# A spectral layer and two expert layers on one core: x in runs of 2 KB, eleven chunks and thirteen decode steps ahead of the second stage

## The chip, the cores and the metric

The kernel runs on one core of a Trainium2 chip. The core has TensorE (PE, the matrix engine), VectorE (DVE), ScalarE (ACT), GpSimd (POOL) and SyncE (SP), which here only issues DMAs, and 16 DMA engines. TensorE writes to PSUM (8 banks of 128 partitions), the other engines compute from PSUM and SBUF. The metric is the device time of one execution in microseconds. The kernel before took 1226.06 us, the median of three runs (1225.86 to 1226.39).

## The reference

x has 2 batches of 3008 positions and 256 features. Each batch goes through a Fourier transform over the positions, a complex linear layer with bias, a soft shrink, and the transform back; then two expert layers follow on all 6016 rows.

```python
X = np.fft.rfft(x, axis=1)
Yr = Xr @ w_r - Xi @ w_i + b_r            # Xr, Xi: real and imaginary part, float32
Yi = Xr @ w_i + Xi @ w_r + b_i
Yr = np.sign(Yr) * np.maximum(np.abs(Yr) - 0.01, 0.0)      # Yi likewise
y = np.fft.irfft(Yr + 1j * Yi, n=3008, axis=1).reshape(6016, 256)
h = y @ moe_w_in;   y = (h - np.tanh(h)) @ moe_w_out        # w_in 256 x 2048, w_out 2048 x 256, float64
h = y @ moe2_w_in;  out = (h * np.clip(h + 3, 0, 6) / 6) @ moe2_w_out
```

## The kernel before

The transform is split as 3008 = 47 x 64 into small matrix products. **First stage (dft_a, L262).** x of a batch lies as 94 rows of 32 positions (a row is 32 KB). A chunk is 4 positions of every row; there are 8 chunks per batch, numbered 0 to 15 over both. dft_a multiplies a chunk from the left with a 96 x 96 matrix (`amt`): four float32 matmuls of 256 columns, two to a PSUM bank; ScalarE copies the two banks back over the chunk (L279) and stores the chunk to `s1` in DRAM from its own queue (L280). The chunks of batch 0 have eight tiles (`xa`), those of batch 1 a ring of three (`xb`).

**Second stage (L674 on, steps t = 0 to 23).** It works on pairs of frequency rows. dft_b (L292) reads a group of `s1` (load_bi, L284, a group serves two steps) and multiplies with `bmt`; ScalarE and VectorE split the result into a high and a low part (`fh`, `fl`); linear (L322) multiplies with the high and low parts of w_r and w_i in three passes, 24 matmuls; the shrink (L337) is three operations of VectorE with ScalarE's copy `sh` (L350) and VectorE's rest `sl` (L354) behind; dft_c (L356) is the third transform, two steps behind linear, and goes to `s2` in DRAM. A step t holds linear(t), dft_c(t-2), dft_b(t+2) and, as long as there are chunks left, the dft_a of one chunk of batch 1: in the kernel before chunks 0 to 7 are done ahead of the stage and chunk 8 + t in steps 0 to 7. Steps 17 to 20 also hold the first dft_d (L394), the fourth transform, for the first tile of the expert layers, and steps 19 to 23 its splits and subtractions (`cmL`, `b22l`, L407, L423).

**The decode (w_steps, L163).** The expert weights come as float64. A generator turns one 256 x 256 block after the other into a high and a low float32 part: raw words in (`raw`, a ring of three), ScalarE's two copies (L172, L173) to `ws`, VectorE's mask (L175), shift (L185), rounding (L197) and, for w_in, four sums (L201 to L205), then ScalarE's high part (L182) and VectorE's low part (L190). Every `next` does one of some six small pieces; each block's third piece issues the load of a later block. In the second stage four calls are made in every step from step 2 on, until 13 blocks are done. The remaining blocks are decoded during the first expert tile.

**Expert layers.** 16 tiles of 376 rows, eight for each layer, each in eight groups of products in three passes; this is most of the time, from some 250 us to the end.

**What sets the order.** The schedule is manual: each engine runs its instructions in the order in which the program writes them. An instruction waits in its queue for what it needs, and everything behind it on its engine waits as well. SyncE issues most DMAs, ScalarE the stores of s1, GpSimd the loads of `cm`, each after a one-element copy to `gate` (L617) that waits for a given tile. Eight semaphores serve the DMAs of SyncE and ScalarE in turn, so an issue can also wait for an earlier transfer on its semaphore.

Of the kernel before, what the change touches and what calls it, by code (L numbers as in the profile page):

```python
# [10 lines left out]
F32 = mybir.dt.float32  # L11
# [3 lines left out]
ACTF = mybir.ActivationFunctionType  # L15
# [72 lines left out]
def spectral_moe_kernel(ctx: ExitStack, tc: tile.TileContext, x, w_r, w_i, b_r, b_i,  # L88
# [14 lines left out]
    y1d = dr.tile([8, 128, 4, 376], F32, name="y1d")  # L103
    s1 = [s1[b].rearrange("k r n d -> k (r n) d") for b in range(2)]
    s2 = [s2[b].rearrange("k r n d -> k (r n) d") for b in range(2)]
    s1w = [s.rearrange("k (q j) d -> (k q) j d", j=32) for s in s1]
    s2w = [s.rearrange("k (q j) d -> (k q) j d", j=32) for s in s2]

    def bank(tag):
# [21 lines left out]
    def alloc_w(nm, c):  # L131
# [3 lines left out]
        W[nm, c] = pl.tile([128, 2, n], F32R, tag=f"w{kind}{c}", name=f"w{kind}{c}")  # L135
        return W[nm, c]

    NDEC, NST = 13, 2
    w_src = {"1i": w1i, "1o": w1o, "2i": w2i, "2o": w2o}
    w_order = [(nm, c) for c in range(8) for nm in ("1i", "1o")]  # L140
    w_order += [(nm, c) for nm in ("2i", "2o") for c in range(8)]
    w_raw = {}
    ptr = {"load": 0, "dec": 0}
# [68 lines left out]
    def w_step():  # L212
        next(w_gen, None)
# [25 lines left out]
    wa_cm = tc.tile_pool(name="wa", bufs=1, side="right")  # L239
    wa = wa_cm.__enter__()  # L240
    x0 = [wa.tile([128, 4, D], F32, name=f"xa{r}") for r in range(8)]
    stores = []

    def load_x(i):
        if i >= 16:
            return
        b, c = divmod(i, 8)
        if b == 0:
            v = x.rearrange("b s d -> (b s) d")[0:96 * 32].rearrange("(r j) d -> r j d", j=32)
            sp.dma_start(out=x0[c][0:96], in_=v[:, 4 * c:4 * c + 4, :])  # L250
        else:
            v = x[b].rearrange("(r j) d -> r j d", j=32)[:, 4 * c:4 * c + 4, :]
            for r0, r1 in ((0, 80), (80, 94)):
                sp.dma_start(out=x1[c % 3][r0:r1], in_=v[r0:r1])

# [5 lines left out]
    def dft_a(i, finish=True):  # L261
        b, c = divmod(i, 8)  # L262
        xt = (x1[c % 3] if b else x0[c])[0:96]
        banks_ = []
        for g in range(2):
            p = bank("acc" if i < 8 and i % 2 else "h")
            pv = p[0:96].rearrange("p (u d) -> p u d", d=D)
            for u in range(2):
                pe.matmul(out=pv[:, u, :], lhsT=amt, rhs=xt[:, 2 * g + u, :], start=True, stop=True)
            banks_.append(pv)  # L270
        if finish:
            dft_a_out(i, banks_)
        return banks_

    def dft_a_out(i, banks_):
        b, c = divmod(i, 8)
        xt = (x1[c % 3] if b else x0[c])[0:96]
        for g in range(2):
            act.activation(out=xt[:, 2 * g:2 * g + 2, :], in_=banks_[g], func=ACTF.Copy)  # L279
        act.dma_start(out=s1w[b][:, 4 * c:4 * c + 4, :], in_=xt)  # L280

    bi_t, xf_t, s_t = {}, {}, {}
    GB = 4
# [1 line left out]
    def load_bi(i):  # L285
        if i >= 2 * K1 // GB:
            return
        b, g = divmod(i, K1 // GB)
        t = bi_ring[i % 3]
        sp.dma_start(out=t, in_=s1[b][g * GB:(g + 1) * GB].rearrange("k p d -> p k d"))  # L290
        bi_t[i] = t
# [316 lines left out]
    with tc.manual_schedule():  # L608
        bv = bm.rearrange("p (k f) -> p k f", k=K1)

        def load_bm(g):
            if g < 6:
                sp.dma_start(out=bmt[:, 4 * g:4 * g + 4, :], in_=bv[:, 4 * g:4 * g + 4, :])

        def load_cm(g, after):
            if g < 6:
                pool.tensor_copy(out=gate[0:1, 0:1], in_=after)  # L617
                for h, t in enumerate((cmH, cmL)):
                    pool.dma_start(out=t[:, 512 * g:512 * g + 512], in_=cm[:, h, 512 * g:512 * g + 512])

        sp.dma_start(out=amt, in_=am)
        for i in range(8):
            load_x(i)
        for r in range(3):
            pool.memset(x1[r][64:96], 0.0)
        dve.memset(three, 3.0)
        lws = []
        for w in (w_r, w_i):
            t = wl.tile([128, 2, D], F32, tag="ly", name="lwf")
            sp.dma_start(out=t, in_=w.rearrange("(h p) d -> p h d", p=128))  # L630
            lws.append(t)
        load_bm(0)
        sp.dma_start(out=dmt, in_=dm)
        for k, w in enumerate((b_r, b_i)):
            sp.dma_start(out=bias[64 * k:64 * k + 64, 0, :],
                         in_=w.rearrange("(o d) -> o d", o=1).broadcast_to([64, D]))
        for i in range(8):
            dft_a(i)
        load_x(8)
        load_bi(0)  # L640
        load_x(9)
        load_bi(1)
        load_bm(1)
        load_cm(0, x0[7][0:1, 3, 0:1])
        load_x(10)
        w_load()
        wa_cm.__exit__(None, None, None)
        wpool["r"] = ctx.enter_context(tc.tile_pool(name="wr", bufs=1, side="right", reuse_waits="tile"))
        for k in range(2):
            split(lwH[:, k], lwL[:, k], lws[k])  # L650
        for j in range(2):
            dft_b(j)
            evict_b_hi(j)
            evict_b_lo(j)
            evict_b_neg(j)
        load_bi(2)
        NP = K1
        a_next = 8
        for t in range(NP):
            linear(t)  # L660
            if t > 1:
                dft_c(t - 2)
            if t + 2 < NP:
                dft_b(t + 2)
            ab = dft_a(a_next, False) if a_next < 16 else None
            if t > 1:
                evict_c(t - 2)
            if t + 2 < NP:
                evict_b_hi(t + 2)
            shrink(t)  # L670
            shrink_hi(t)
            if t + 2 < NP:
                evict_b_lo(t + 2)
            if t == NP - 1:  # L674
                first = first_group()
                next(first)
            if t + 2 < NP:
                evict_b_neg(t + 2)
            for _ in range(2):
                if t > 1 and ptr["dec"] < NDEC:  # L680
                    w_step()
            shrink_lo(t)
            for nm in {20: ("b11", "b21"), 21: ("t1",), 22: ("t2", "b22")}.get(t, ()):
                op_lo(0, nm)
            if t == 20:
                op_sub(T1, B12, B11, dve)
            if t == 21:
                op_sub(T2, B22, T1, dve)
            if ab:
                dft_a_out(a_next, ab)  # L690
                a_next += 1
            flush_stores()
            if t % 2 == 0:
                load_bm(t // 2 + 2)
                load_cm(t // 2 + 1, s_t[t][0].bitcast(F32)[0:1, 0, 0:1])
            if t > 0:
                load_x(10 + t)
            if t in (0, 1):
                w_load()
            if t % 2 == 1:  # L700
                load_bi((t + 1) // 2 + 2)
            for _ in range(NST):
                if t > 1 and ptr["dec"] < NDEC:
                    w_step()
            if t == 14:
                load_din(0, din0)
            if t == 15:
                load_din(1, x1[2])
            if t in (17, 18):
                dft_d(0, t - 17, "h")  # L710
            if t in (19, 20):
                dft_d(1, t - 19, "h")
            for nm in {19: ("b11", "b21"), 20: ("t1",), 21: ("t2", "b22")}.get(t, ()):
                op_hi(0, nm)
            if t == 22:
                op_sub(T3, B22, B12)
                op_sub(T4, B21, T2)
# [110 lines left out]
```

## Time and profile before

| | |
|---|---|
| profiled execution, own time | 1225.78 us |
| its span, first to last instruction | 1224.0 us |
| TensorE busy | 1183.5 us (97%) |
| VectorE busy | 962.5 us (79%) |
| ScalarE busy | 880.8 us (72%) |
| GpSimd busy | 158.7 us (13%) |
| DMA traffic | 96.51 MB, mean 79 GB/s |

The profile is one execution of the program. Busy shares are means over stages that are limited by different things, so the table says little by itself; the rows further down take the stages apart. A row of the timeline gives start and duration of instructions, and in brackets how long the engine had been idle and what ended that. A row of the table of windows gives, for a stretch of time, what each engine was busy with in it, TensorE's granted clock as a share of full speed, the DMA engines' busy share and the rate.

### The profile page before, as it was taken

How to read it: one execution, taken by the hardware profiler on the slowest of the kernel's cores; microseconds unless marked ns; L12 is line 12 of the kernel's file. 1: busy time of each engine (PE TensorE's matmuls, PEld its weight loads, DVE VectorE, ACT ScalarE, POOL GpSimd, SP SyncE). 2: the span in 40 equal slices, each digit the busy share in tenths (PEclk: the TensorE clock that was granted, in tenths of full speed). 3: DMA queues.
4: the chain of work that ended last, by engine and by line, in shares of the span. 5: the costliest groups of instructions: out<-in, count | busy, mean ns of one | idle time of the engine just before them, and what ended most of it. 6: DMA issues, size and time to landing. Idle time of an engine off the chain costs nothing.

```text
span 1224.0 us, 20880 instructions
## 1 busy us (share of the span) xinstructions
PE 1183.5 (97%) x7824; PEld 1163.0 (95%) x7824; DVE 962.5 (79%) x1808; ACT 880.8 (72%) x1836; POOL 158.7 (13%) x164
## 2 busy tenths in 40 slices
PE   5899979899999999999999999999999999999998
PEld 3799969899999999999999999999999999999998
DVE  0479988888888888888778787878787878787875
ACT  3477767777787777777777777777777777777775
POOL 1000010201102020202021320202020202020200
PEclk9899989999999999999999999999999999999999
DMA  9896522232212122211104530101010101001000
GB/s 269 239 334 209 185 86 67 99 106 74 74 49 98 66 69 69 61 60 44 43 1 166 185 130 1 51 1 52 1 52 1 52 1 35 18 22 31 10 18 26
DMA packets 47797, 96.51 MB, mean 79 GB/s; under 512 B 4448, under 2 KB 27488, under 8 KB 47696
## 3 DMA queue, kind: packets, MB, share of 16 engines
q1 hardware_dynamic: 41728, 74.08, 18.8%
q0 software_dynamic: 4032, 14.68, 3.9%
q10 hardware_dynamic: 1936, 6.42, 1.4%
q8 instruction: 61, 1.00, 0.3%
q14 instruction: 40, 0.33, 0.1%
HBM read 58.73 MB, written 36.44 MB: 78 GB/s over the span
## 4 chain that ended last, share of the span: by engine, by line
PE 76%; DVE 10%; ACT 10%; issue 3%; DMA 2%; SPq 0%; ACTq 0%; DVEq 0%
PE acc L119 13%; PE acc L121 13%; PE acc L120 13%; PE al L119 7%; PE al L120 6%; PE al L121 6%; PE be L121 3%; PE be L120 3%; PE be L119 3%; ACT gh L115 2%; DVE g L440 2%; PE ga L398 2%; PE ga L120 2%; PE ga L121 2%; PE ga L119 1%
## 5 line engine op out<-in xcount | busy, mean ns | idle before, releaser
L116 DVE TENSOR_TENSOR gl<-g,gh 128x376 fp32r<-128x376 f32 x509 | 290.4, 571 | 149.7 <-ACT gh L115 122.1
L115 ACT ACTIVATE gh<-g 128x376 fp32r<-128x376 f32 x509 | 263.5, 518 | 185.5 <-DVE g L443 91.8
L121 PE MATMUL acc<-wo,gl 128*128 128x256 f32 (+1 forms) x768 | 215.9, 281 | 0.0
L120 PE MATMUL acc<-wo,gh 128*128 128x256 f32 (+1 forms) x768 | 215.8, 281 | 0.0
L119 PE MATMUL acc<-wo,gh 128*128 128x256 f32 (+1 forms) x768 | 215.7, 281 | 0.0
L119 PE MATMUL acc<-gh,wo 128*128 128x376 f32 x512 | 173.2, 338 | 0.0
L121 PE MATMUL acc<-gh,wo 128*128 128x376 f32 x512 | 171.0, 334 | 0.0
L120 PE MATMUL acc<-gl,wo 128*128 128x376 f32 x512 | 170.7, 333 | 0.0
L120 PEld LDWEIGHTS acc<-wo,gh 128*128 128x128 f32 (+1 forms) x768 | 143.0, 186 | 0.0
L121 PEld LDWEIGHTS acc<-wo,gl 128*128 128x128 f32 (+1 forms) x768 | 143.0, 186 | 0.0
L119 PEld LDWEIGHTS acc<-wo,gh 128*128 128x128 f32 (+1 forms) x768 | 142.8, 186 | 0.0
L407 POOL TENSOR_TENSOR bmt<-bmt 128x376 f32<-128x376 f32 x62 | 73.9, 1192 | 521.5 <-ACT bmt L400 396.8
L443 DVE SCALAR_TENSOR_TENSOR g<-e,c 128x376 f32<-128x376 f32 x192 | 119.3, 621 | 12.5 <-ACT e L442 7.9
L442 ACT ACTIVATE e<-c,three 128x376 f32<-128x376 f32 x192 | 116.7, 608 | 8.0 <-DVE c L589 7.2
L440 DVE TENSOR_TENSOR g<-c,e 128x376 f32<-128x376 f32 x189 | 113.9, 603 | 8.2 <-ACT e L439 6.0
L423 POOL TENSOR_TENSOR cmL<-bmt,cmH 128x376 fp32r<-128x376 f32 x60 | 66.1, 1102 | 325.8 <-ACT cmH L418 322.5
L439 ACT ACTIVATE e<-c 128x376 f32<-128x376 f32 x189 | 97.5, 516 | 7.9 <-DVE c L589 7.7
L119 PEld LDWEIGHTS acc<-gh,wo 128*128 128x128 f32 x512 | 96.4, 188 | 0.0
L120 PEld LDWEIGHTS acc<-gl,wo 128*128 128x128 f32 x512 | 96.3, 188 | 0.0
L121 PEld LDWEIGHTS acc<-gh,wo 128*128 128x128 f32 x512 | 96.1, 188 | 0.0
L119 PE MATMUL al<-cmH,wi 128*128 128x376 f32 x256 | 87.8, 343 | 6.3 <-ACT bi_all L538 2.9
L579 ACT ACTIVATE s<-be 128x376 f32<-128x376 f32 x127 | 61.9, 487 | 39.8 <-PE be L121 39.4
(164 smaller groups left out, 2830.8 us busy)
## 6 DMA issues: line engine op xcount, KB each, us to landing
raw<-in_moe_w_in_dram SPq DMA_DIRECT2D x16, 512.0 KB, 5.0
raw<-in_moe_w_out_dram SPq DMA_DIRECT2D x16, 512.0 KB, 4.4
w2id<-wout SPq DMA_DIRECT2D x8, 896.0 KB, 4.3
wi<-w2id POOLq DMA_DIRECT2D x8, 896.0 KB, 4.9
bi_all<-s SPq DMA_DIRECT2D x12, 512.0 KB, 6.5
y1d<-y SPq DMA_DIRECT2D x32, 188.0 KB, 2.0
bmt<-y1d SPq DMA_DIRECT2D x8, 752.0 KB, 4.9
s<-co SPq DMA_DIRECT2D x23, 256.0 KB, 5.5
```

The source lines that it names most:

```text
L115: act.activation(out=hi, in_=src, func=ACTF.Copy)
L116: (lo_eng or dve).tensor_tensor(out=lo, in0=src, in1=hi.bitcast(F32), op=ALU.subtract)
L119: pe.matmul(out=out_ap, lhsT=lh, rhs=rh, start=start, stop=False, **kw)
L120: pe.matmul(out=out_ap, lhsT=lh, rhs=rl, start=False, stop=False, **kw)
L121: pe.matmul(out=out_ap, lhsT=ll, rhs=rh, start=False, stop=stop, **kw)
L407: eng.tensor_tensor(out=out, in0=a, in1=b, op=ALU.subtract)
L423: (eng or dve).tensor_tensor(out=l, in0=OPS[nm][0], in1=h.bitcast(F32), op=ALU.subtract)
L439: act.activation(out=e, in_=src, func=ACTF.Tanh)
L440: dve.tensor_tensor(out=g, in0=src, in1=e, op=ALU.subtract)
L442: act.activation(out=e, in_=src, func=ACTF.Relu, bias=three)
L443: dve.scalar_tensor_tensor(out=g, in0=e, scalar=6.0, in1=src, op0=ALU.min, op1=ALU.mult)
L579: act.activation(out=s5, in_=be, func=ACTF.Copy)
```

## The change

- **Runs of 2 KB.** A chunk is now 2 + 2 positions of every row, 16 positions apart, instead of 4 neighbouring ones. Loads of x and stores to s1 move two runs of 2 KB, 16 KB apart, where they moved one of 4 KB.
- **Evictions.** For chunks 0 to 10 ScalarE copies one bank and VectorE the other.
- **Warm-up.** Four matmuls on a zeroed tile stand ahead of the first dft_a.
- **Eleven chunks ahead.** Chunks 8, 9 and 10 are done ahead of the second stage (A0 = 11), chunks 11 to 15 in steps 0 to 4.
- **Thirteen decode steps ahead.** Nine calls stand around chunks 8 to 10, four behind the first two dft_b. So that only tiles are used that exist by then, the order of blocks is now 1i0, 1i1, 1o0, 1o1.
- **Loads.** The first raw load and chunks 8 and 9 are issued ahead of the first stage's wait, behind w_r and w_i; chunk 10, the second raw and group 2 of s1 close behind the first group; `dm` later. The gate of the first cm load names chunk 8's tile.
- The split of w_r and w_i stands behind chunk 4.

```diff
-    s1w = [s.rearrange("k (q j) d -> (k q) j d", j=32) for s in s1]
+    s1w = [s.rearrange("k (q h j) d -> (k q) h j d", h=2, j=16) for s in s1]
...
+    A0 = 11
-    w_order = [(nm, c) for c in range(8) for nm in ("1i", "1o")]
+    w_order = [("1i", 0), ("1i", 1), ("1o", 0), ("1o", 1)]
+    w_order += [(nm, c) for c in range(2, 8) for nm in ("1i", "1o")]
...
-            sp.dma_start(out=x0[c][0:96], in_=v[:, 4 * c:4 * c + 4, :])
+            sp.dma_start(out=x0[c][0:96], in_=v[:, :, 2 * c:2 * c + 2, :])
...
-            act.activation(out=xt[:, 2 * g:2 * g + 2, :], in_=banks_[g], func=ACTF.Copy)
-        act.dma_start(out=s1w[b][:, 4 * c:4 * c + 4, :], in_=xt)
+            if g and i < A0:
+                dve.tensor_copy(out=xt[:, g], in_=banks_[g])
+            else:
+                act.activation(out=xt[:, g], in_=banks_[g], func=ACTF.Copy)
+        act.dma_start(out=s1w[b][:, :, 2 * c:2 * c + 2, :], in_=xt)
...
+        warm = ca.tile([128, 256], F32, name="warm")
+        dve.memset(warm, 0.0)
+        for _ in range(4):
+            p = bank("h")
+            pe.matmul(out=p[:, 0:256], lhsT=warm[:, 0:128], rhs=warm, start=True, stop=True)
...
+        w_load()
+        load_x(8)
         load_bm(0)
-        sp.dma_start(out=dmt, in_=dm)
+        load_x(9)
...
         for i in range(8):
             dft_a(i)
-        load_x(8)
+            if i == 4:
+                for k in range(2):
+                    split(lwH[:, k], lwL[:, k], lws[k])
         load_bi(0)
-        load_x(9)
+        load_x(10)
         load_bi(1)
+        w_load()
         load_bm(1)
-        load_cm(0, x0[7][0:1, 3, 0:1])
-        load_x(10)
+        load_cm(0, x1[0][0:1, 1, 1, 0:1])
+        load_bi(2)
         w_load()
+        sp.dma_start(out=dmt, in_=dm)
+        for i in range(8, A0):
+            w_step()
+            dft_a(i)
+            w_step()
+            w_step()
...
-        for k in range(2):
-            split(lwH[:, k], lwL[:, k], lws[k])
+        load_x(11)
         for j in range(2):
             dft_b(j)
             evict_b_hi(j)
             evict_b_lo(j)
             evict_b_neg(j)
-        load_bi(2)
+            w_step()
+            w_step()
...
-        a_next = 8
+        a_next = A0
...
-            if t > 0:
-                load_x(10 + t)
-            if t in (0, 1):
-                w_load()
+            load_x(12 + t)
```

Three places in the engines' orders. SyncE's queue at the start of the second stage, before (bi_all is a group of s1, xb a chunk of batch 1 in two parts, bmt and bias are constants, raw a block of expert weights):

```order
L635 DMA bias<-in_b_i_dram 64x256
L254 DMA xb_98<-in_x_dram 80x1024
L254 DMA xb_98<-in_x_dram 14x1024
L290 DMA bi_all<-s_0_60 128x4x256
L254 DMA xb_99<-in_x_dram 80x1024
L254 DMA xb_99<-in_x_dram 14x1024
L290 DMA bi_all<-s_0_60 128x4x256
L613 DMA bmt<-in_bm_dram 128x512
L254 DMA xb_100<-in_x_dram 80x1024
L254 DMA xb_100<-in_x_dram 14x1024
L156 DMA raw<-in_moe_w_in_dram 128x2x256
```

The same place of the changed kernel; xb_98 at the end is chunk 11:

```order
L296 DMA bi_all<-s_0_60 128x4x256
L257 DMA xb_100<-in_x_dram 80x2x512
L257 DMA xb_100<-in_x_dram 14x2x512
L296 DMA bi_all<-s_0_60 128x4x256
L158 DMA raw<-in_moe_w_in_dram 128x2x256
L619 DMA bmt<-in_bm_dram 128x512
L296 DMA bi_all<-s_0_60 128x4x256
L158 DMA raw<-in_moe_w_out_dram 128x2x256
L663 DMA dmt<-in_dm_dram 96x94
L158 DMA raw<-in_moe_w_out_dram 128x2x256
L158 DMA raw<-in_moe_w_in_dram 128x2x256
L257 DMA xb_98<-in_x_dram 80x2x512
```

Chunks 8 and 9 have moved ahead of the first s1 group, and four raw loads now stand between it and the load of chunk 11.

ScalarE's queue from the last chunk of batch 0 to the first linear, before (lwH is the split of w_r and w_i, fh and fl the split of dft_b's result):

```order
L280 DMA s_0_60<-xa_112 96x1024
L115 ACTIVATE lwH<-lwf 128x512 x2
L308 ACTIVATE fh<-al 128x4x128
L309 ACTIVATE fh<-al 128x4x64
L320 ACTIVATE fl<-fl 128x4x64
```

And of the changed kernel (ws and wi are decode, xb_98 to xb_100 chunks 8 to 10):

```order
L174 ACTIVATE ws<-raw 128x512
L175 ACTIVATE ws<-raw 128x512
L285 ACTIVATE xb_98<-al 96x512
L286 DMA s_1_61<-xb_98 192x1x512
L285 ACTIVATE xb_99<-al 96x512
L286 DMA s_1_61<-xb_99 192x1x512
L174 ACTIVATE ws<-raw 128x512
L175 ACTIVATE ws<-raw 128x512
L184 ACTIVATE wi_275<-ws 128x896
L285 ACTIVATE xb_100<-al 96x512
L286 DMA s_1_61<-xb_100 192x1x512
L314 ACTIVATE fh<-al 128x4x128
```

Behind the last store of batch 0, chunks 8 to 10 and the copies of two raw blocks now stand ahead of the first fh.

VectorE's queue from step 20 to step 21, before (ly, lc, sl are the shrink, cmL and bmt the next stage's splits, ws and wo decode):

```order
L344 TENSOR_TENSOR ly<-ly,lc 128x512
L315 TENSOR_TENSOR fl<-be,fh 128x4x128
L185 SCALAR_TENSOR_TENSOR ws<-ws,raw 128x512
L190 TENSOR_TENSOR wo_1618<-ws,wo_1618 128x512
L354 TENSOR_TENSOR sl<-ly,sh 128x512
L423 TENSOR_TENSOR cmL<-bmt,cmH 128x376 x2
L407 TENSOR_TENSOR bmt<-bmt 128x376
L197 ISA ws<-ws 128x1024
L201 TENSOR_TENSOR ws<-ws 128x128
L202 TENSOR_TENSOR ws<-ws 128x128
L342 TENSOR_TENSOR ly<-acc,bias 128x512
```

And of the changed kernel:

```order
L350 TENSOR_TENSOR ly<-ly,lc 128x512
L321 TENSOR_TENSOR fl<-be,fh 128x4x128
L360 TENSOR_TENSOR sl<-ly,sh 128x512
L429 TENSOR_TENSOR cmL<-bmt,cmH 128x376 x2
L413 TENSOR_TENSOR bmt<-bmt 128x376
L348 TENSOR_TENSOR ly<-acc,bias 128x512
```

The five decode instructions of that step are gone from here; in the changed kernel the last ones of the stage stand in step 18.

## Rows read from the trace of the kernel before

**Rows 1.** Table of windows: stages of the kernel.

```profile
core 0: us, PE busy (x) PEld busy (x) DVE busy (x) ACT busy (x) POOL busy (x), PEclk, DMA share, GB/s
...
22.50:35.50 13.00, 0.00 (x0) 0.00 (x0) 1.29 (x2) 3.31 (x6) 1.34 (x3) 0.59 0.94 299
35.50:91.50 56.00, 55.13 (x398) 51.40 (x399) 37.77 (x66) 36.54 (x73) 5.21 (x12) 0.97 0.90 289
91.50:152.20 60.70, 60.07 (x511) 59.61 (x510) 58.45 (x109) 44.07 (x88) 1.23 (x3) 1.00 0.64 200
152.20:174.60 22.40, 15.72 (x107) 14.59 (x105) 19.64 (x36) 13.01 (x27) 2.42 (x2) 0.92 0.32 94
174.60:250.00 75.40, 68.00 (x374) 64.19 (x375) 64.62 (x126) 54.76 (x116) 11.40 (x9) 0.96 0.28 88
250.00:1224.00 974.00, 967.82 (x6377) 961.24 (x6375) 780.67 (x1471) 720.93 (x1517) 134.15 (x128) 1.00 0.15 51
```

**Rows 2.** Timeline of the head: start, duration, engine, line, what; idle time before it.

```profile
5.71 0.71 PE L269 MATMUL al<-xa,amt 96*96 96x256 f32 x1 [5.71 <-DMA xa<-in_x_dram]
...
24.14 1.08 ACT L279 ACTIVATE xa<-acc 96x512 f32<-96x512 f32 x2 [0.44 <-ACT xa L279]
25.25 0.31 ACTq L280 DMA_DIRECT2D s<-xa  x1
...
28.76 0.40 SPq L290 DMA_DIRECT2D bi_all<-s  x1
...
35.54 2.05 PE L301 MATMUL al<-bmt,bi_all 128*128 128x128 f32 x8 [13.05 <-issue]
37.62 0.60 ACT L308 ACTIVATE fh<-al 128x512 fp32r<-128x512 f32 x1 [10.87 <-PE al L301]
...
38.77 0.36 PE L119 MATMUL acc<-lwH,fh 128*128 128x256 f32 x1
```

**Rows 3.** DMA issues: count, KB each, us to landing; last row over the span.

```profile
s<-xa ACTq DMA_DIRECT2D x1, 384.0 KB, 3.5
...
bi_all<-s SPq DMA_DIRECT2D x1, 512.0 KB, 6.7
...
raw<-in_moe_w_in_dram SPq DMA_DIRECT2D x1, 512.0 KB, 9.2
...
raw<-in_moe_w_in_dram SPq DMA_DIRECT2D x16, 512.0 KB, 5.0
```

**Rows 4.** Table of windows: stretches of the head.

```profile
4.00:14.00 10.00, 8.29 (x26) 5.84 (x27) 0.00 (x0) 4.36 (x7) 0.00 (x0) 1.00 1.04 255
...
24.00:28.00 4.00, 0.00 (x0) 0.00 (x0) 1.29 (x2) 2.23 (x4) 1.34 (x3) 0.62 0.96 356
...
30.00:40.00 10.00, 4.43 (x23) 4.23 (x24) 0.69 (x1) 1.62 (x4) 0.00 (x0) 0.57 0.97 255
```

**Rows 5.** Windows from one dft_b to the next: in steps 7, 8, 18; then one dft_b.

```profile
86.01:92.18 6.17, 6.17 (x48) 5.77 (x48) 5.14 (x9) 5.27 (x11) 0.00 (x0) 1.00 1.05 367
92.18:96.62 4.44, 4.44 (x40) 4.44 (x40) 3.75 (x8) 2.41 (x5) 1.23 (x3) 1.00 0.48 136
138.66:143.99 5.33, 5.33 (x48) 5.33 (x47) 5.23 (x12) 2.94 (x6) 0.00 (x0) 1.00 0.47 120
...
92.18 0.89 PE al L301 x8
```

**Rows 6.** Window of ws alone (DVE, ACT); then VectorE's groups by form, 35 to 175 us.

```profile
35.00:175.00 140.00, 37.41 (x68) 26.70 (x41) 0.98 0.69 218
...
L342 DVE TENSOR_TENSOR ly<-acc,bias 128x512 f32<-128x512 f32 x24 | 16.5, 686 | 7.3 <-PE acc L121 6.1 <-DMA bmt<-in_bm_dram 1.1
...
L343 DVE TENSOR_SCALAR lc<-ly 128x512 f32<-128x512 f32 x24 | 10.3, 427 | 0.8
...
L423 DVE TENSOR_TENSOR cmL<-bmt,cmH 128x376 fp32r<-128x376 f32 x4 | 2.9, 743 | 0.0
```

**Rows 7.** VectorE's first shrink instruction: step 4, and all from 90 us on.

```profile
65.56 0.69 DVE L342 TENSOR_TENSOR ly<-acc,bias 128x512 f32<-128x512 f32 x1 [0.63 <-PE acc L121]
...
L342 DVE TENSOR_TENSOR ly<-acc,bias x16: 671/684/692, 91.5 to 171.5; 128x512 f32<-128x512 f32 x16
```

More of the change, by code (lines that the diff above doesn't have):

```diff
@@ L241, in spectral_moe_kernel @@
     x0 = [wa.tile([128, 4, D], F32, name=f"xa{r}") for r in range(8)]
+    x0, x1 = ([t.rearrange("r (h j) d -> r h j d", h=2) for t in xs] for xs in (x0, x1))
     stores = []
@@ L248, in load_x @@
         if b == 0:
-            v = x.rearrange("b s d -> (b s) d")[0:96 * 32].rearrange("(r j) d -> r j d", j=32)
-            sp.dma_start(out=x0[c][0:96], in_=v[:, 4 * c:4 * c + 4, :])
+            v = x.rearrange("b s d -> (b s) d")[0:96 * 32].rearrange("(r h j) d -> r h j d", h=2, j=16)
+            sp.dma_start(out=x0[c][0:96], in_=v[:, :, 2 * c:2 * c + 2, :])
         else:
-            v = x[b].rearrange("(r j) d -> r j d", j=32)[:, 4 * c:4 * c + 4, :]
+            v = x[b].rearrange("(r h j) d -> r h j d", h=2, j=16)[:, :, 2 * c:2 * c + 2, :]
             for r0, r1 in ((0, 80), (80, 94)):
@@ L268, in dft_a @@
             for u in range(2):
-                pe.matmul(out=pv[:, u, :], lhsT=amt, rhs=xt[:, 2 * g + u, :], start=True, stop=True)
+                pe.matmul(out=pv[:, u, :], lhsT=amt, rhs=xt[:, g, u, :], start=True, stop=True)
             banks_.append(pv)
@@ L707, in spectral_moe_kernel @@
             if t == 15:
-                load_din(1, x1[2])
+                load_din(1, x1[2].rearrange("r h j d -> r (h j) d"))
             if t in (17, 18):
```

## The prediction, made before the changed kernel ran

> **What bounds the kernel now.** I read the table of stages first [rows 1]. Its last row says where nothing is to be had: from 250 us on TensorE is busy 967.8 of 974.0 us, and the change touches nothing there. Before that TensorE stands still for 13.0 us between 22.5 and 35.5 us and for 6.7 us (22.40 - 15.72) between 152.2 and 174.6 us, beside the first 5.7 us, in which it waits for x [rows 2]. From 91.5 to 152.2 us it is busy, but so is VectorE: 58.45 of 60.70 us, while the DMAs are down to a share of 0.64. That is the stage in which VectorE sets the pace, as the rows on the shrink will show. From 35.5 to 91.5 us TensorE is busy 55.13 of 56.00 us with the DMAs at 0.90.
>
> The timeline of the head [rows 2] gives the chain there. The first chunk of x reaches TensorE at 5.71 us. The store of the eighth chunk is issued by ScalarE at 25.25 us; SyncE waits for all eight stores and issues the first load of the second stage at 28.76; the first dft_b starts at 35.54, and the first linear at 38.77. The times to landing [rows 3] fill the gaps: 3.5 us for that store, 6.7 for that load. All along the DMAs are full: share 1.04 from 4 to 14 us, 0.96 from 24 to 28, 0.97 from 30 to 40 [rows 4].
>
> **The change part by part.** I write Tb for the issue of the first load of s1 (28.76 us now), and take the kernel in three pieces: up to the first linear, from there to step 4, and from step 4 to step 23, the last of the second stage.
>
> *Up to the first linear.* The four warm-up matmuls run while TensorE waits for x, so they cost nothing; if x came at once they would cost their own time, a few tenths each by the 0.71 us of the first cold matmul record [rows 2]. One chunk of dft_a costs 6.17 - 4.44 = 1.73 us at full clock, the difference of a step with it and one without [rows 5]. Eight of them from 5.71 us, with 0.8 us lost to the rest of the clock's rise, end at 20.3 us, where ScalarE's last eviction now ends near 25.2. One eviction on each of ScalarE and VectorE, side by side, leaves some 0.7 us, so the last store is issued near 21.0. With 3.5 us to landing that makes Tb 24.7 at best. Against it stands the traffic: 0.52 MB of weights, 0.39 MB of the tenth chunk and 0.52 MB of cm (its gate now waits only for chunk 8's load) are put ahead of or beside the stores. At 356 GB/s [rows 4] these 1.43 MB take 4.0 us, less about 1 us of room, so Tb is 31.7 at worst. I take 28, near the present value, because the DMAs are full there: what TensorE gains, the stores lose.
>
> The Trainium skill ("DMA: Bandwidth & Descriptors", section "Issuing engines are not separate DMA queues") says that transfers of all issuing engines end on the same 16 DMA engines and interleave, so a store on ScalarE's queue has no path of its own past SyncE's loads. That speaks against moving loads up; by it alone Tb would be at the worst value.
>
> Behind Tb, ScalarE's order decides. The decode step's two copies of the second weight block (raw) stand ahead of the tenth chunk's eviction and of the first fh. This raw is issued behind the loads of s1 group 0, chunk 10 and s1 group 1, about 2.2 us after Tb (four issues of 0.3 to 0.4 us and their gaps), and lands 5.0 us (the median of such loads) to 9.2 us (the first of them now) later [rows 3]; the 9.2 had a bm load and a longer chunk queue in front, so I take 7.3, between the two, or Tb + 9.5. Then ScalarE runs three decode copies (26.70 / 41 = 0.65 each [rows 6]), one eviction (half of 1.08) and one store issue (0.31 [rows 2]), 2.8 us, and the first linear follows 1.15 us after fh starts, as it does now (37.62 to 38.77). That is Tb + 13.5 (11.2 to 15.4) or 41.5 us, against 38.77: **2.7 us later** (35.9 to 47.1). The three chunks (5.2 us of TensorE) and the 13 decode steps lie in this gap, hidden by the DMAs; if the loads came at once they would cost their 5.2 us, and the decode steps nothing, since they are on other engines.
>
> *First linear to step 4.* Both kernels have a chunk of dft_a in each of these steps, so TensorE's work is the same 26.8 us (38.77 to 65.56 [rows 7]). New is that SyncE issues chunk 11's load behind three raw loads, of which the last waits until VectorE has decoded raw: it comes near Tb + 10.7 and lands some 6 us after, one microsecond or so later than TensorE wants it. And the DMAs must bring as much as before in less time: from Tb to chunk 15 I count 12.3 MB (six chunks 2.3, five stores 2.0, four s1 groups 2.1, bm 0.8, cm 1.6, raw 3.1, s2 0.4). At the stage's mean 289 GB/s [rows 1] that is 42.6 us, so chunk 15 at 70.6, where TensorE would be ready at 41.5 + 26.8 = 68.3. At 356 GB/s it would be 62.6 and no stall. I take **2.5 us** of stall (0 to 7).
>
> *Step 4 to step 23.* A step of VectorE is four operations of 0.69 and one of 0.43 us, 3.2 us. The stage makes 81 calls of the decode's generator, four to a step from step 2 on; its instructions on ws take VectorE 37.41 us, so four calls add 1.85 [rows 6] (the mask on raw, 0.4 us in every sixth call, is not in that row). The sum is 5.05 us, and the starts of the shrink say the same: there are sixteen from 91.5 to 171.5 us [rows 7], the first is step 8, the thirteenth stands at 152.2, and 60.7 / 12 = 5.06. TensorE needs 4.44 without dft_a and 5.33 with dft_d [rows 5]. So now VectorE is the later one, and at the end of the stage it also has the operand splits and subtractions of the next stage (such as cmL, 0.74 each [rows 6]) and the decode's last steps at once; there are the 6.7 us of idle TensorE.
>
> After the change 13 of the 81 calls are done. The decode then ends with step 18 and not in step 22. Step 4 still has a chunk, 6.17 us; from step 5 to 19 VectorE needs 14 x 5.06 = 70.8; from 19 to 23 its four steps without decode, 12.8 us, and seven splits and subtractions less what TensorE's lead hides of them, make 15.6, an estimate from these rows. That is 92.6 us. TensorE's own sum is 6.17 + 12 x 4.44 + 4 x 5.33 (dft_d in steps 17 to 20) + 4.44 + 3.55 (the last has no dft_b, 0.89 [rows 5]) = 88.8, so it is not the later one. Now it is 171.5 - 65.6 = 106.0. **13.4 us less** (11 to 16.5). Of this 5.2 us are the three chunks of dft_a, and the rest is TensorE's idle time, so it does not exceed what is there. Late next is VectorE still, through steps 5 to 18.
>
> *The rest.* After step 23 both kernels have the same 13 weight blocks decoded, and the order is the same. I take 0 (-2 to +2: TensorE is idle for 75.40 - 68.00 = 7.4 us between 174.6 and 250 [rows 1], and I let a shift in time open or close a quarter of it). Runs of 2 KB for x and the stores I take at 0 for the DMAs' rate.
>
> **The sum**: +2.7 + 2.5 - 13.4 = -8.2 us. The profiled execution took 1225.78 us, 0.3 below the median of the runs; 1225.8 - 8.2 = 1217.6, and I say **1217**.
>
> **The rivals.** *Runs of 2 KB make the loads quick.* x comes at 255 GB/s from 4 to 14 us, in rows 32 KB apart, while the DMAs move 356 at 24 to 28 us [rows 4]. With half runs 16 KB apart the 3.1 MB of x might come at that rate: 8.8 us for 12.3. TensorE sets the pace behind it, but the queue of stores starts 3.5 us earlier, so Tb is near 24.7, the stall at step 0 to 4 goes, and the time is about 1217.6 - 3.3 - 2.5 = 1212. For it: the weights' loads, also 2 KB runs with a pitch of 16 KB, run in stretches with a high rate; against it: no row shows x so read, and 30 to 40 us is as slow as the start with chunk loads among others.
> The Trainium skill (the same page, "Latency and other measured facts") reports lower rates for row pitches at large powers of two, and calls its cause an inference; its smallest pitch is 512 KB, so it gives no figure here.
>
> *The DMAs become the bound of the first steps: slower.* Place: steps 0 to 4, where chunks 11 to 15 and their stores must pass. If the DMAs move what they move from 30 to 40 us, 255 GB/s [rows 4], the 12.3 MB take 48.2 us, and with Tb at 31.7 chunk 15 comes at 79.9 where TensorE, whose first linear is then at 45.2, would be ready at 72: a stall of 8. Then the sum is 6.4 + 8 - 13.4 = +1, or 1227. It decides from a mean rate under some 260 GB/s. For it: the share of 0.97 at only 255 GB/s, with the same kinds of loads. Against it: 367 GB/s from 86 to 92 us [rows 5], and a mean of 289 that has idle time in it.
>
> *The decode is not what holds VectorE.* If ScalarE's chain (fh behind the dft_d evictions) sets the end of the stage, the splits stay late and only the three chunks count: -5.2 + 2.7 + 2.5 = 0, or 1226. For it: steps 20 and 21 have ScalarE waits among VectorE's; against it: VectorE is busy 19.64 of 22.40 us there [rows 1].
>
> **How the numbers follow.** The forecast (second stage shorter by 11 to 16.5, head and first steps later by 2 to 9) has 0.65, with its own range 1211 to 1223; quick loads 0.15 (1207 to 1214); DMA-bound first steps 0.12 (1220 to 1229, slower in 0.08 of it); ScalarE's chain 0.08. About 0.2%, 2.5 us, can be told from no change. Faster: 0.65 + 0.15 + 0.03 + 0.02 = 0.85; same 0.06; slower 0.09. The range that leaves out 2 in 10 is 1208.5 to 1224.
>
> **What would show it.** In the changed profile: the first x matmuls at 0.38 us a record; Tb between 25 and 32; the second raw copy on ScalarE waiting for its DMA just before the first fh, and the first linear near 41 us; a wait for chunk 11 at step 0; steps of 5.1 us through step 18 and no decode on VectorE behind it; TensorE's idle time between the last steps mostly gone. The forecast is wrong if the first linear starts after 47 us, if steps 8 to 23 stay 5.3 us apart on the mean (80.0 / 15), or if the stretch after step 23 is over 2 us longer or shorter.

## The result: 1238.9 us, slower by 1%

The changed kernel took 1238.88 us, the median of four runs (1237.91 to 1240.63), beside 1226.1 for the kernel before: a ratio of 1.0105, interval 1.009 to 1.012. I had predicted 1217 and faster. The profiled execution took 1238.9 us, its span is 1237.1, 13.1 longer than before.

| stretch, us | before | predicted | after | after less before |
|---|---|---|---|---|
| start to first linear | 38.77 | 41.5 | 46.60 | +7.8 |
| first linear to the shrink of step 4 | 26.8 | 29.3 | 38.4 | +11.6 |
| shrink of step 4 to that of step 23 | 106.0 | 92.6 | 99.2 | -6.8 |
| shrink of step 23 to the end | 1052.5 | 1052.5 | 1052.9 | +0.4 |

The gain in the third stretch is there, and half of what I expected; the first two stretches cost nearly four times what I gave them.

The table of windows of the changed kernel, with the columns and boundaries of [rows 1]:

```profile
22.50:35.50 13.00, 7.02 (x16) 4.19 (x16) 4.54 (x9) 3.58 (x6) 1.34 (x3) 0.59 0.92 290
35.50:91.50 56.00, 43.15 (x272) 38.28 (x272) 28.48 (x50) 26.16 (x52) 3.97 (x9) 0.85 0.76 245
91.50:152.20 60.70, 57.31 (x475) 55.98 (x474) 54.85 (x103) 39.34 (x80) 2.79 (x6) 1.00 0.66 202
152.20:174.60 22.40, 22.03 (x189) 21.79 (x188) 20.28 (x38) 17.07 (x34) 0.43 (x1) 1.00 0.51 159
...
71.20:77.80 6.60, 0.25 (x3) 0.09 (x2) 3.63 (x7) 3.44 (x7) 0.00 (x0) 0.87 0.94 340
77.80:84.80 7.00, 7.00 (x32) 5.91 (x33) 0.00 (x0) 1.19 (x2) 0.00 (x0) 0.64 0.63 212
```

From 35.5 to 91.5 us TensorE is now idle for 12.9 us (56.00 - 43.15) where it was idle for 0.9, while the DMAs are less busy than before (0.76 for 0.90). So this is not a lack of DMA rate. The last two rows are one piece of it: TensorE does nearly nothing for 6.6 us, and in the seven that follow its granted clock is 0.64 of full speed in the mean, so part of them runs at the lower of its two levels, 1.2 GHz: the matmuls behind the wait are slow as well.

The timeline of the changed kernel's head, columns as in [rows 2], ScalarE's, SyncE's and TensorE's rows put in order of time:

```profile
8.93 0.65 ACTq L286 DMA_DIRECT2D s<-xa  x1
...
17.60 0.56 ACTq L286 DMA_DIRECT2D s<-xa  x1
...
25.60 0.56 ACTq L286 DMA_DIRECT2D s<-xa  x1
...
33.41 0.38 SPq L296 DMA_DIRECT2D bi_all<-s  x1
...
39.29 1.99 PE L272 MATMUL al<-xb,amt 96*96 96x256 f32 x4 [3.41 <-DMA xb<-in_x_dram]
...
42.24 0.66 ACT L174 ACTIVATE ws<-raw 128x512 f32<-128x512 f32 x1 [7.40 <-DMA raw<-in_moe_w_in_dram]
42.78 1.92 PE L307 MATMUL al<-bmt,bi_all 128*128 128x128 f32 x8
...
45.95 0.60 ACT L314 ACTIVATE fh<-al 128x512 fp32r<-128x512 f32 x1 [1.15 <-PE ga L307]
...
46.60 0.39 PE L119 MATMUL acc<-lwH,fh 128*128 128x256 f32 x1 [0.66 <-ACT fh L314]
```

Two engines stand at a load here: TensorE until 39.29 us at chunk 10, with the first dft_b behind it, and ScalarE until 42.24 at the second raw block, with the first fh behind it. Both loads were issued behind the first load of s1 at 33.41. The first store was issued at 8.93, the fourth at 17.60; the last left at 25.60, later than the 25.25 of [rows 2], and landed after 7.8 us instead of 3.5 [rows 3]:

```profile
s<-xa ACTq DMA_DIRECT2D x1, 384.0 KB, 7.8
```

Next the waits of SyncE from 50 to 75 us and of TensorE from 47 to 90 (who waited for whom: us, times, longest), and SyncE's issues around them:

```profile
SPq L158 <- DVE ws L187: 13.1, 1, 13.1
...
PE al L272 <- DMA xb<-in_x_dram: 6.3, 1, 6.3
PE be L272 <- DMA xb<-in_x_dram: 1.9, 1, 1.9
```

```profile
54.42 0.46 SPq L296 DMA_DIRECT2D bi_all<-s  x1
68.00 0.37 SPq L158 DMA_DIRECT2D raw<-in_moe_w_out_dram  x1
...
69.49 1.53 SPq L257 DMA_DIRECT2D xb<-in_x_dram  x2
```

SyncE stands for 13.1 us at the load of a raw block, whose tile VectorE frees only when the decode goes on in step 2. Chunk 14's load, at 69.49, is queued behind it, and TensorE waits 6.3 us for chunk 14. The wait of 1.9 us is for chunk 11.

Last, the shrinks of steps 4 to 23 (the answer to [rows 7]), and VectorE's wait at the mask from 91 to 170 us:

```profile
L348 DVE TENSOR_TENSOR ly<-acc,bias x20: 679/683/692, 85.0 to 184.2; 128x512 f32<-128x512 f32 x20
...
DVE raw L177 <- ACT ws L174: 5.2, 5, 1.0
```

### The profile page after: what moved, and what is told of

It reads as the page before. It is cut to its first block, busy times and chain, and to the rows that moved or that the text cites. A ratio compares the mean times of both kernels' runs of the same rounds, so it can differ in the third digit from the quotient of the medians.

```text
span 1237.1 us, 20913 instructions
## 1 busy us (share of the span) xinstructions
PE 1193.0 (96%) x7832; PEld 1167.9 (94%) x7832; DVE 970.1 (78%) x1820; ACT 874.6 (71%) x1825; POOL 158.4 (13%) x164
## 4 chain that ended last, share of the span: by engine, by line
PE 76%; DVE 10%; ACT 8%; DMA 4%; issue 2%; SPq 0%; ACTq 0%; DVEq 0%
PE acc L119 13%; PE acc L121 13%; PE acc L120 13%; PE al L119 7%; PE al L120 6%; PE al L121 6%; PE be L121 3%; PE be L120 3%; PE be L119 3%; ACT gh L115 2%; DVE g L446 2%; PE ga L404 2%; PE ga L121 2%; PE ga L120 2%; PE ga L119 2%
## 5 line engine op out<-in xcount | busy, mean ns | idle before, releaser
L445 ACT ACTIVATE e<-c 128x376 f32<-128x376 f32 x189 | 97.6, 516 | 7.9 <-DVE c L595 7.7
```

Of the source, the lines that this page charges most:

```text
L445: act.activation(out=e, in_=src, func=ACTF.Tanh)
```

## The experiments

Times are medians; the kernel before took 1224.9 to 1225.8 us beside them, and the ratios are to it, so kernels of different experiments are compared by ratio. A stretch or a start named without a row is read from the trace of that run; times in the head differed by some 2 us between single executions (six kernels with the same instructions up to the first load of s1 issue it between 31.7 and 34.0: the changed one, e4, f1, f2, f4, g1), so there I count only what two runs agree on or what the engines' order says.

**The parts of the head and SyncE's order, each alone.**

**e1, runs of 4 KB again** (batch 0's load; batch 1's and the stores likewise).
```diff
-            sp.dma_start(out=x0[c][0:96], in_=v[:, :, 2 * c:2 * c + 2, :])
+            sp.dma_start(out=x0[c][0:96].rearrange("r h j d -> r (h j) d"), in_=v[:, 4 * c:4 * c + 4, :])
```


> The changed kernel with x and s1 in runs of 4 KB again, and nothing else undone. Theory A, the runs of 2 KB cost the head: in the changed kernel the packets of x took 144 to 153 ns for 2 KB where 4 KB took some 265, and a store's issue on ScalarE 0.56 us for 0.31. Then the first load of s1 is issued near 30 us instead of 33.41, the first linear comes near 43.5 instead of 46.64, and the time is 3 to 5 us under the changed kernel's 1238.9. Theory B, the loads put ahead of the stores (raw, chunks 8 and 9) cost the head: the first load of s1 stays within 1 us of 33.4 and the time within 2 us of 1238.9.

1236.49 us, ratio 1.0093 (1.0079 to 1.0107); first load of s1 at 30.63 us, first linear at 44.95. Theory A for the place, and a smaller price than it said: 1.5 us by the ratios, whose intervals overlap, so this price alone is not clear of noise.

**e2, the kernel before with runs of 2 KB** (the reverse edit on it).

> The kernel before with x and s1 in runs of 2 KB, and nothing else. Theory A (the runs cost the head): the first load of s1 at 31 to 32 us instead of 28.76, the time 1229 to 1231. Theory B (the loads ahead do): 28.3 to 29.3, and 1226 within 1.5 us.

1227.13 us, ratio 1.0021 (1.0012 to 1.003). The first load of s1 came at 31.52, as A said, but the first linear at 38.75, unchanged: the load took 4.0 us to land instead of 6.7. The time, 2.6 us over the kernel before, lies in B's range. In the trace 1.8 us are lost later, in steps 5 to 11, where TensorE's waits for loads are 2.0 us in all instead of 0.7. The last store left at 27.25 instead of 25.25: its eight issues on ScalarE take 0.56 us each instead of 0.31.

**e3, raw and chunk 9 loaded behind the first load of s1.**
```diff
-        w_load()
-        load_x(8)
         load_bm(0)
-        load_x(9)
...
+        load_x(8)
         load_bi(0)
+        load_x(9)
+        w_load()
         load_x(10)
```


> The changed kernel with the first raw load and chunk 9's load moved behind the first load of s1; chunk 8's stays ahead of it, as in the kernel before. Theory B (loads ahead of the stores cost the head): 0.9 MB less stand in front of the stores, at 255 GB/s 3.5 us, so the first load of s1 is issued near 29.5 to 30.5 us instead of 33.41. Of that the first linear keeps some 2 us (44 to 45), since chunk 9 and the decode come later by themselves, and the time is about 1236 to 1237. Theory A (the runs of 2 KB do): the first load of s1 stays above 32 us and the first linear at 46.6 or later, time 1239 or more.

1242.14 us, ratio 1.0148 (1.0132 to 1.0164): slower still. The first load of s1 was issued at 30.88, 2.5 us sooner, and the first linear came at 47.18, no sooner. Both theories fall: when that load is issued does not decide. What decides must be behind it, and what stands there are the loads of chunks 9 and 10 and of raw, which were now later; f2, f4 and g1 below test them.

**e4, chunk 12 + t loaded first in its step.**
```diff
             ab = dft_a(a_next, False) if a_next < 16 else None
+            load_x(12 + t)
...
-            load_x(12 + t)
```


> The changed kernel with the load of chunk 12 + t issued at the beginning of step t, ahead of the step's raw load, instead of behind it. In the changed kernel SyncE waits from 54.9 to 68.0 us for a free raw tile, chunk 14's load is issued behind that at 69.49, and TensorE stands still for 6.5 us at dft_a(14). Theory C (this order on SyncE costs the first steps): chunk 14's load is issued at 50 to 56 us, the wait of dft_a(14) falls under 1 us, step 4's shrink comes at 76 to 78 us instead of 85.06, and the time is 6 to 9 us under 1238.9, near 1231. Rival D (the DMAs can't bring it sooner, or the decode, which is what the raw tile waits for, is late by itself): the shrink of step 4 comes 1 to 3 us sooner and the time is 1236 or more.

1228.58 us, ratio 1.0037 (1.0025 to 1.005), 8 us less than the changed kernel by the ratios and 10.8 by the spans: theory C. Chunk 14's load was issued at 59.47, later than I expected (it waits for the store of chunk 11), and TensorE's waits from 47 to 90 us shrank to

```profile
PE be L272 <- DMA xb<-in_x_dram: 0.8, 1, 0.8
PE acc L121 <- DVE fl L321: 0.5, 1, 0.5
```

and the 34 matmuls of dft_a(14) and the linear behind it ran at full clock, in 4.55 us; step 4's shrink came at 74.8 instead of 85.0.

```profile
69.80:74.35 4.55, 4.55 (x34) 4.16 (x33) 3.08 (x6) 4.11 (x9) 0.00 (x0) 1.00 1.00 363
```

**The decode's phase, and the two halves of the change.** All four start from e4.

**f1, twelve steps ahead.**
```diff
             evict_b_neg(j)
             w_step()
-            w_step()
+            if j == 0:
+                w_step()
```


> The changed kernel with chunk 12 + t loaded first in step t (as in e4_x_first, 1228.58 us) and with twelve decode steps ahead instead of thirteen. Theory P, the phase of the decode against the steps costs the stage: with thirteen ahead the two copies of a w_out block fall on the first call of a step, the mask behind them waits for ScalarE, and each third step takes 6.06 us (mean 5.28); with twelve they fall where the kernel before has them, and steps 7 to 18 take 5.06 in the mean. Twelve times 0.22 is 2.6 us: about 1226. Rival Q, ScalarE is late in these steps by its own load, wherever the copies stand: steps stay at 5.2 to 5.3 and the time at 1228 to 1229.

1224.9 us, ratio 0.9993 (0.9984 to 1.0001), under e4 by 5 us by the ratios: theory P. Its shrinks of steps 10 to 19, and below them ten of the changed kernel, steps 7 to 16:

```profile
L348 DVE TENSOR_TENSOR ly<-acc,bias x10: 681/682/684, 105.5 to 150.0; 128x512 f32<-128x512 f32 x10
```
```profile
L348 DVE TENSOR_TENSOR ly<-acc,bias x10: 681/684/689, 103.1 to 150.6; 128x512 f32<-128x512 f32 x10
```

Nine steps are three periods of the decode (a w_in and a w_out block take twelve calls, four to a step): 44.5 us or 4.94 a step here, 47.5 or 5.28 there. VectorE's wait for ScalarE at the mask is gone. Every kernel here with thirteen steps ahead has 6.06 us in each third step to the end of the decode (the changed one, e1, e3, e4, f2, f4); of those with twelve (f1, g1, g2, g3) or none (the kernel before, e2, f3, g4) none has this pattern.

**f2, decode steps behind the first fh.**
```diff
         for i in range(8, A0):
-            w_step()
+            if i < 10:
+                w_step()
             dft_a(i)
-            w_step()
-            w_step()
+            if i < 10:
+                w_step()
+            if i < 9:
+                w_step()
...
             evict_b_neg(j)
-            w_step()
-            w_step()
+            for _ in range(4):
+                w_step()
```


> e4_x_first with the decode steps from the sixth on (the sixth holds ScalarE's two copies of the second raw block, for which ScalarE waited 9.04 us, to 42.44) moved behind the first fh; thirteen steps are done ahead of the stage as before. Theory R, ScalarE's order sets the first linear: fh starts when the first dft_b is done, near 42.2 instead of 45.65, the first linear comes at 43 to 43.5 instead of 46.34, and the time is 2.5 to 3.3 us under e4_x_first's 1228.58. Rival H, the DMAs set it (busy 0.93 from the start to the first linear, as in the kernel before): the first linear comes sooner, but TensorE then waits for chunk 11 and the second fl, and what is gained is given back by step 1; time within 1 us of 1228.58.

1229.62 us, ratio 1.0031 (1.0021 to 1.0041): no gain clear of noise. The first linear stood at 46.22 (46.30 in e4), but not for H's reason: ScalarE was ready and waited for the first dft_b, which TensorE began at 43.95, behind chunk 10, for which it had waited until 40.46.

**f3, no decode ahead** (e4 less its `w_step` and `w_load` ahead of the stage, `w_load` in steps 0 and 1 as in the kernel before).

> e4_x_first without the decode ahead: no decode steps and no raw loads ahead of the second stage (the loads come where the kernel before has them), eleven chunks ahead as in the changed kernel. Theory H, bytes put ahead of the first linear cost DMA time: 1.5 MB of raw less at 0.30 MB per us is 5 us, so the first linear is at 41 to 42.5 instead of 46.34 (38.77 in the kernel before, which stores three chunks less by then). The stage has the decode to its end again, steps 5 to 19 at 5.06 and the last four as in the kernel before, so that step 4 to step 23 takes some 101.7 us. Sum: +3 at the head and -4.3 in the stage against the kernel before, 1223 to 1225 where that has 1224.9. Rival R, ScalarE's wait for raw is what sets the head: first linear near 43, and the chunks, not raw, hold it.

1227.48 us, ratio 1.0014 (1.0006 to 1.0022), above the 1223 to 1225 that I expected. First dft_b at 41.33, behind chunk 10 again, and at the lower clock; first linear at 44.61. H's bytes would have given 41 to 42.5. The end of the stage is that of the kernel before, 24.8 us from step 19 to step 23.

**f4, eight chunks ahead.**
```diff
-    A0 = 11
+    A0 = 8
-        load_x(11)
...
-            load_x(12 + t)
+            load_x(10 + t if t else 16)
```


> e4_x_first with only eight chunks ahead (chunks 8 to 15 in steps 0 to 7, as in the kernel before), and the thirteen decode steps and their loads ahead as in the changed kernel. Theory H: three stores (1.2 MB, 4 us) less ahead of the first linear, which ScalarE's decode copies still hold back: 42 to 43.5 instead of 46.34. In the stage steps 0 to 7 are TensorE's as in the kernel before, steps 8 to 18 take 5.28 (the phase of thirteen), the last four as in the changed kernel 17.7, so that from step 8 to step 23 it is 76 instead of 80.0. Sum against the kernel before: +4 - 4 = 0, 1224 to 1226. If the decode ahead were worth nothing (the end of the stage is held by ScalarE's chain), the stretch from step 19 to step 23 stays near 24.7 and the time is 1229 or more.

1233.36 us, ratio 1.0064 (1.005 to 1.0078), far over the 1224 to 1226 of theory H. The first dft_b began at 37.49, with the landing of its own load, but ScalarE stood at raw: first fh at 43.82, first linear at 44.44. From step 19 to step 23 it took 17.7 us. The first shrink, behind the decode on VectorE, was already 8.5 us later than before, and step 5 with 10.07 us and the steps of 6.06 took most of what the end of the stage gave back. What made step 5 so long no run separates; in the trace ScalarE waits 1.6 us there for a store of s2, TensorE stands for 2.2 us, and the DMAs are full from 74.7 to 84.8 us (share 1.09).

**Both waits away, and the counter-tests.**

**g1, ten chunks and five decode steps ahead of the first fh** (f1 with f2's order and `A0 = 10`).

> f1_x_first_twelve (1224.9 us) with ten chunks ahead instead of eleven and the decode steps from the sixth on behind the first fh, so that neither TensorE nor ScalarE has, ahead of the first linear, work on a load that is issued behind the first load of s1. Theory R, two waits in the order of the engines set the first linear, chunk 10's on TensorE and raw's on ScalarE (f2 took away only the second, f4 only the first, and neither gained): the first dft_b starts with its own load at 37.5 to 38.5 us, the first linear comes at 41 to 42.5 instead of 45.2; the chunk costs the stage 1.7, and the time is about 1223. Rival H, the bytes moved ahead set it: the first linear stays at 44 or later, or TensorE waits for chunks 10 to 12 in the first steps, and the time is 1226 or more.

1221.49 us, ratio 0.9968 (0.9956 to 0.9981). Its timeline:

```profile
36.56 2.05 PE L307 MATMUL al<-bmt,bi_all 128*128 128x128 f32 x8 [1.12 <-DMA bi_all<-s]
...
38.64 0.60 ACT L314 ACTIVATE fh<-al 128x512 fp32r<-128x512 f32 x1 [4.24 <-PE al L307]
...
39.97 0.56 PE L119 MATMUL acc<-lwH,fh 128*128 128x256 f32 x1
```

Theory R: the first dft_b waits for its own load alone, and the first linear comes at 39.97, 6.6 us sooner than in the changed kernel and only 1.2 later than before. Taking away one wait had left it at 46.2 (f2) and 44.4 (f4).

**g2, g1 with e1's runs of 4 KB.**

> g1_nothing_behind_tb with x and s1 in runs of 4 KB. If the runs of 2 KB cost what e1 and e2 show (some 2 us each), it is 1.5 to 2.5 us under g1, about 1221; if they cost only where TensorE waits for chunk 10, it is within 1 us of g1.

1218.12 us, ratio 0.9939 (0.9927 to 0.9951), 3.4 under g1: the fastest kernel here, faster than the kernel before and the changed one. The runs of 2 KB cost 1.5 (e1, within the noise), 2.6 (e2) and 3.6 us (here) by the ratios.

**g3, the kernel before with its decode begun in step 0.**
```diff
             ab = dft_a(a_next, False) if a_next < 16 else None
+            if t > 0:
+                load_x(10 + t)
...
-            if t > 0:
-                load_x(10 + t)
...
-            for _ in range(NST):
-                if t > 1 and ptr["dec"] < NDEC:
+            for _ in range({0: 2, 1: 4}.get(t, NST + (t < 8))):
+                if ptr["dec"] < NDEC:
```


> The kernel before with its decode begun earlier inside the stage: two calls in step 0, four in step 1, five instead of four in steps 2 to 7 (twelve in all, so that the phase of the later calls stays), and the load of chunk 10 + t issued first in step t. Nothing is moved ahead of the first linear. Theory V, the decode is what holds VectorE and so the end of the stage: the stretch from step 19 to step 23 takes 17.7 us as in the changed kernel instead of 24.7, the first linear stays at 38.8, and the time is 1217.5 to 1219.5 where the kernel before has 1225. Rival D, the DMAs (share 0.90 in steps 0 to 9) can't bring the raw blocks earlier: TensorE waits for chunks or VectorE for raw in steps 1 to 7, and the time is 1222 or more.

1221.36 us, ratio 0.9967 (0.9955 to 0.998). The last five shrinks of the stage (steps 19 to 23) and, for comparison, the kernel before's:

```profile
L342 DVE TENSOR_TENSOR ly<-acc,bias x5: 675/684/686, 147.0 to 165.5; 128x512 f32<-128x512 f32 x5
```
```profile
L342 DVE TENSOR_TENSOR ly<-acc,bias x5: 677/685/687, 146.8 to 171.5; 128x512 f32<-128x512 f32 x5
```

18.5 us for 24.7: theory V for the place. The time lies between its range and D's, and rival D has its part, since a step 5 of 9.56 us instead of 7.43 gives some of the gain back.

**g4, the kernel before with the warm-up and evictions on both engines.**
```diff
-            act.activation(out=xt[:, 2 * g:2 * g + 2, :], in_=banks_[g], func=ACTF.Copy)
+            if g and i < 8:
+                dve.tensor_copy(out=xt[:, 2 * g:2 * g + 2, :], in_=banks_[g])
+            else:
+                act.activation(out=xt[:, 2 * g:2 * g + 2, :], in_=banks_[g], func=ACTF.Copy)
```


> The kernel before with the four warm-up matmuls and one of a chunk's two evictions on VectorE for chunks 0 to 7, and nothing else. Theory H, the DMAs are full from 4 us to the first linear: the last store is issued at 21 to 23 us instead of 25.25, but the first load of s1 and the first linear come within 0.7 us of 28.76 and 38.77, and the time is within 1 us of the kernel before. Rival, the chain through ScalarE's evictions sets the head: the first linear comes 2 to 4 us sooner, and the time is 2 to 4 us under the kernel before.

1226.92 us, ratio 1.0004 (0.9995 to 1.0013): no difference in the time, as H says. The last store was issued at 24.08, later than H's 21 to 23, and the first load of s1 at 30.47, 1.7 us later than before where H allowed 0.7; the first linear came at 38.26. One thing moved besides: the load of cm, whose gate waits for what VectorE now copies, was issued at 20.7 instead of 25.4 us, ahead of the last three stores.

## Why the prediction was wrong

**Term 1, up to the first linear: +7.8, not +2.7 (range to 47.1).** The part from the first load of s1 on held: 46.60 - 33.41 = 13.2 us, where I had 13.5. Two things were wrong. The issue of that load came at 33.41, not 28, and past my worst case of 31.7. TensorE was done with the eight chunks at 20.2 us, as I had reckoned, but the last store left at 25.60 and not near 21.0. I took the copies for what holds ScalarE; what I left out is that a store's issue waits for an earlier transfer on its semaphore. The kernel before issues its fourth store at 19.14, when the second has landed (12.78 + 6.3), and g4 its fourth at 16.76, when the first has (8.53 + 8.1); the two share a semaphore each time. In the changed kernel the fourth waits until 17.60 in the same way. This is read from the traces; no run takes it away. So g4, with faster copies, has its first load of s1 at 30.47 and gains nothing, and the runs of 2 KB and the loads ahead come on top (e1 and e3, each without one of them, have it at 30.6 and 30.9, under the 31.7 to 34.0 of the six with both). The Trainium skill's rule ("DMA: Bandwidth & Descriptors", section "Issuing engines are not separate DMA queues") pointed to the late end of the range, and the traces agree: the last store took 7.8 us to land behind the loads (8.0 and 7.5 in e4 and f1, with the same head), 5.0 in e3, where raw and chunk 9 come later.

The weightier error is that I named one gate only. I found ScalarE's raw on the path and took the three chunks as "hidden by the DMAs"; but chunk 10's load is issued behind the first load of s1 too, and it holds TensorE's own queue with the first dft_b in it. Either gate alone keeps the first linear at 44 to 46 us (f4, f2); g1 takes away both and has it at 40.

**Term 2, first linear to step 4: +11.6, not +2.5 (0 to 7). This is the step that failed most.** I counted bytes over rate, 12.3 MB at 289 GB/s, and found a stall of 2.5. The mean rate fell to 245 with the DMAs idle a quarter of the time: what was late was the issue, not the transfer. In the kernel before, SyncE waits for a raw tile in the same place, 6.1 us at its raw load at 58.67:

```profile
SPq L156 <- DVE ws L185: 6.1, 1, 6.1
```

But there chunk 10 + t is loaded in step t and used in step t + 2. With eleven chunks ahead chunk 12 + t is used in step t + 1, so the same order leaves one step less; and thirteen decode steps ahead fill the three raw tiles, of which none comes free until the decode goes on in step 2. The diff showed both. I had seen the order for chunk 11 only, and its wait of 1.9 us is near the one that I reckoned for it. 6.3 us is the wait for chunk 14, and 2.4 more is the slow clock behind the second: the 7.00 us row above, where e4 takes 4.55 for the same work. e4 gives back 8 us by the order alone. My rival of DMA-bound first steps had the stall and its size (8 us) by the wrong mechanism, so its size was luck; its condition, a rate under 260 GB/s, was met only as a consequence.

**Term 3, step 4 to step 23: -6.8, not -13.4.** The mechanism stood: the decode ended with step 18, steps 19 to 23 took 17.7 us where I had an estimate of 15.6, and g3 and f3 show from both sides that the decode is what holds the end (18.5 with it early, 24.8 with it late). Of the 6.6 us that are missing, 4.5 lie in steps 4 to 19 (81.5 us, where I had 77.0) and 2.1 in the last four. The first part is the 5.06 us for a step. It was a mean over twelve steps that held one of 6.05, in which VectorE waited 0.6 us for an fh; the other eleven take 4.97 (97.6 to 152.2), so by itself this would have made the time shorter. What failed is that it takes the four calls as equal work wherever they fall: shifted by thirteen, the copies of a w_out block stand at a step's first call with the mask right behind, VectorE waits 1.03 us for ScalarE in each third step, and the mean is 5.28. f1 shifts by one call, saves 5 us, and takes 76.2 us for steps 4 to 19, so this is the place and the price. The 2.1 us: I compared TensorE's sum with VectorE's over all nineteen steps, 88.8 and 92.6, and not over the last four. There TensorE is busy 17.22 us of 17.72 and VectorE 15.95, near my 15.6: TensorE is the later one, by its own rows some 17.8 us (5.33 + 2 x 4.44 + 3.55). No run tests this.

**The rest, 0: right (+0.4).** **Runs of 2 KB at 0: wrong for the time,** by 2.6 and 3.6 us (e2, g2). For the DMAs' rate, of which I had said it, no loss is shown: from 4 to 14 us the changed kernel's trace has 230 GB/s for the 255 of [rows 4], but the eight other kernels with runs of 2 KB have 242 to 267, and the five with 4 KB 251 to 268. What is seen in every trace is the longer issue, 0.56 us for 0.31 on ScalarE; how much of the price it explains is open. The rival of quick loads falls too, since no run comes near 356. The rival of ScalarE's chain is refuted by g3.

**The sum.** From the changed kernel to g2 four edits take off 0.0166 of the ratio, 20 us (the second gives back a decode step, the third a chunk, the fourth the runs of 2 KB): SyncE's order 8.3, the phase 5.4, the two gates 3.1, the runs 3.6. What is left, 1218.1, is near my 1217, but partly by luck: g2's stretches are 0.1 us shorter, 2.1 longer, 9.5 shorter and 0.2 shorter than before, where I had +2.7, +2.5, -13.4 and 0, and it has ten chunks and twelve decode steps ahead and runs of 4 KB.

## What to carry to other kernels

When work is moved ahead, list for every engine what then stands in its queue before the first instruction of the old path, and for each of those when its load is *issued*; two such gates hide one another, and here only the experiment that took away both showed what they cost. Count a prefetch's lead in steps, before and after, along with what stands ahead of it in the issuing queue, before dividing bytes by a rate: a mean rate that falls while the DMAs stand idle points at a queue, not at a bound. And where a generator is woven into a loop, moving it by a few calls changes which of its pieces meet; look at the pattern over its period and not at the mean.

## What the runs showed of the hardware

- A transfer in runs of 2 KB costs its issuing engine 0.56 to 0.6 us instead of 0.31 to 0.43 (x on SyncE, the stores on ScalarE). That it also moves its bytes more slowly is not shown: 242 to 267 GB/s from 4 to 14 us in eight kernels and 230 in the changed one, against 251 to 268 with 4 KB.
- The issue of a store waits on its engine for the landing of an earlier transfer on the same semaphore: the fourth store of g4 went out at 16.76 us, 0.1 behind the landing of the first, though its chunk's two copies were done at 13.6.
- After a wait of 6.3 us TensorE ran part of the matmuls that followed at the lower clock, mean 0.64 over 7 us; in e4, where the wait is gone, the same work ran at 1.00. The wait so cost more than its length, here by 2.4 us.
